# A two-part kernel on one core: first rows, GpSimd's DMA queue and the order of the last tables

## The chip, the cores and the metric

The kernel runs on one core of a Trainium2 chip. Its time is the device time of one execution in microseconds (us); for several runs the median is given. The core has five engines, each with its own program order: PE (TensorE: matmuls, transposes), DVE (VectorE), ACT (ScalarE), POOL (GpSimd) and SP (SyncE, which here only issues DMAs). SP, ACT and POOL issue DMAs, each in its own order: an instruction that waits holds up all that stands behind it on its engine. Sixteen DMA engines move the data for all of them.

## What is computed

The output has two halves side by side. The left half is an attention layer with a memory that is carried from segment to segment; the right half is a long convolution whose kernel comes from a state space model.

```python
# a: 64 segments of 32 rows, one after the other, 32 heads of 128
for s in range(n_seg):
    h = concatenate([mem, x[:, s*32:(s+1)*32]])          # 8 + 32 rows
    q, k, v = h @ Wq, h @ Wk, h @ Wv
    p = softmax(where(mask, q k^T * scale, -1e9))
    o = (p v) @ Wo
    mem = o[:, :8];  outs.append(o[:, 8:])
# b: convolution of u (2048 x 1024) with a kernel of 128 modes per column
K = real(sum_n C_n * exp(dt*A_n * l) * dt*B_n)           # l = 0..2047
y = irfft(rfft(pad(K)) * rfft(pad(u)))[:2048] + u * Dskip
return concatenate([a, b], axis=-1)
```

## The kernel before

**Part b comes first** (`part_b`, L699). It works in four stages, and parts of part a that do not depend on the recurrence are woven into them.

1. The parameter stage (the loop over `PAR`, L944) computes from A, B, C and log_dt the logarithms of the modes, split into three bfloat16 parts each, and stores them to the DRAM tensor `PB` (`part_put`, L883). The words of `PAR` set the order on every engine: T/c turn x's last rows, F/f build Fourier matrices `MF`, P/e are projections of part a (`Ahead.projections`, L140) and their evictions.
2. The loop over f from 0 to 15 (L1308) makes the tables and the convolution kernel's values, one block of 64 columns a pass. The words of `FIRST` (pass 0) and `ORDER` (the others) give the order: X..p and X..t are matmuls of the parameters, which `load_par` (L1029) brings from `PB` into one of two tiles `pt`, four DMAs a pass, one pass ahead, called in `exp_` (word E0); E is the exponential on ACT, n, S, b, C, w, gi, gr the sines and products on ACT and DVE, K and x the values and their copy into `KxT`. Woven in are U (`side`, L997: u's spectra on PE; every fourth eviction ends in `classes`, six operations on POOL and a 1 MB store to `Ud`), M (turned matrices, a store to `MId` from POOL), P (projections), R (`other_rows`, L114: x's other rows turned and stored to `VXd` by SP, L135).
3. After the passes 7 and 15, `put_values` (L1065) queues 44 stores of half of the kernel's values to `Kd` in a list `late`. One is taken out at each E (L1245), eight a pass, and issued by SP; those of the second half go out together after the loop (L1385), by POOL except the four largest, which stay with SP. In the tail (L1344 to L1389) the last tables are finished, and the turned columns `G` of the first blocks are built (`build`, L1162) and multiplied with the values that `load_k` (L1079) reads back from `Kd`.
4. The loop over b from 0 to 15 (L1509) multiplies the spectra block by block (`pointwise`, L1408) with u's, which `load_u` (L1196) loads through SP, and from b=4 on transforms back (`inverses`). At b=2 SP loads the second half of `Kd`. Part a's weights are loaded in the same loop (`resident`).

**Part a** (`part_a`, L266) then runs its 64 segments, streaming the weights that do not fit into SBUF; it is not touched.

The projections' outputs go by way of a list of their own, `Ahead.late`: `PKd` stores (eight for each finished group, L210) and `VXd<-PVd` copies, of which up to `burst` are issued before each eviction (L188, L201). PSUM tiles for the woven work come from `take` (L729), three buffers in turn. Where GpSimd's DMAs keep their descriptors is set small (`SCRATCH = 512`, L1580), to leave the room to weights.

Of the kernel before, what the change touches and what calls it, by code (L numbers as in the profile page):

```python
# [74 lines left out]
class Ahead:  # L75
# [38 lines left out]
    def other_rows(self, take, pool, ident):  # L114
# [11 lines left out]
        for b in range(NB):  # L126
# [5 lines left out]
            def evict(copy, b=b, pt=pt):  # L132
                xst = pool.tile([128, 4, self.KC, self.XM], BF16, name="xst", tag="xst", bufs=1)
                copy(out=xst[:].rearrange("p s k r -> p k s r"), in_=pt[:, :, 0:n].rearrange("p k (s r) -> p k s r", r=self.XM))
                nc.sync.dma_start(out=self.VXd[4 * b:4 * b + 4, :, 256:].rearrange("s p f -> p s f"), in_=xst[:].rearrange("p s k r -> p s (k r)"))  # L135
                if b + 2 < NB:
                    load(b + 2)
            yield evict

    def projections(self):  # L140
# [13 lines left out]
        self.burst = 0  # L154
# [20 lines left out]
        for i, (m, t, c) in enumerate(slices):  # L175
# [3 lines left out]
            for j in range(2):  # L179
                a = take([128, 512], F32, "pro")  # L180
                if m == "v":
# [5 lines left out]
                    def evict(copy, a=a, t=t, c=c, j=j):  # L187
                        for _ in range(min(self.burst, len(late))):  # L188
                            (late.pop(0) or skip)()
# [5 lines left out]
                else:  # L195
# [4 lines left out]
                    def evict(copy, a=a, m=m, t=t, g=g, h=h2 + j, mo=mo):  # L200
                        for _ in range(min(self.burst, len(late))):  # L201
# [6 lines left out]
                        def out():  # L208
                            for r in range(8):
                                late.append(lambda r=r: nc.sync.dma_start(out=PKd[8 * r:8 * r + 8, :, mo:mo + 128].rearrange("s p f -> p s f"),  # L210
                                                                          in_=st[:, 8 * r:8 * r + 8].rearrange("p s a b c -> p s (a b c)")))
# [457 lines left out]
def bcast_front(ap, n):  # L669
# [20 lines left out]
FIRST = ("X0p' X0t' U0 X1p E0 n0 X1t u0 U1 X2p E1 n1 X2t u1 P0 X3p E2 n2 X3t p0 U2 X4p E3 n3 X4t u2 U3 X5p E4 n4 X5t u3 P1 X6p E5 n5 X6t p1 "  # L690
         "X7p E6 n6 X7t E7 n7 P2 S0 p2 S1 P3 R p3 r M m P4").split()
# [3 lines left out]
       "f20 lo6/ F21 q4 P12 at e11/ b1 F22 P13 b2 f21 f22 b3 e12 F23 hi4 P14 q3 f23 e13 s4 hi3 F24 F25 e14/ P15 mi4 s3 f24 lo4 mi3 F26 P16 "  # L695
       "f25 lo3 e15 f26 F27 F28 f27 P17 e16 F29 e17 P18 f28 f29 F30 F31 f30 P19 f31 e18 P20 e19 e20").split()


def part_b(ctx, tc, u, A_re, A_im, B_re, B_im, C_re, C_im, log_dt, Dskip, out_b, ahead, copies, residents, first_state):  # L699
# [20 lines left out]
    v.memset(magic[:], MAGIC)  # L720
    ahead.open(ahead.ctx)
# [4 lines left out]
    ps_k = ctx1.enter_context(tc.tile_pool(name="b_psk", bufs=3, space=PSUM, side="right"))  # L726
# [11 lines left out]


# [13 lines left out]
    with tc.tile_pool(name="b_par", bufs=1) as par, tc.tile_pool(name="b_parh", bufs=2) as parh, \  # L753
# [129 lines left out]
        def part_put(k, i):  # L883
            q, row = {"1": (0, 0), "4": (0, 3), "2": (1, 0), "3": (1, 3), "6": (1, 6)}[k]
            sy.dma_start(out=PB[q][row + i].rearrange("(p t) n -> p t n", t=8), in_=parts[k, i][:])
# [23 lines left out]
        def ttx(word, eng, *args):  # L909
# [16 lines left out]
            "rp": powers_rows, "rt": phase_rows}  # L926
# [102 lines left out]
    def load_par(sb, eng=gp):  # L1029

        for q in range(2):
            n = 4 * PARTS[q]
            for h in range(2):
                eng.dma_start(out=par_t[sb % 2][ROW0[q] + n * h:ROW0[q] + n * h + n],
                             in_=PB[q][:].rearrange("c (q g s h e) n -> q s h c g e n", q=2, g=4, s=8, h=2)[sb // 8][sb % 8][h])
        return par_t[sb % 2]

# [24 lines left out]
    def put(out, in_):  # L1062
        late.append(lambda eng=sy: (sy if out.shape[1] == 32 else eng).dma_start(out=out, in_=in_))

    def put_values(sb):  # L1065
        kx = KxT["t"]
        for g in range(4):
            dsl = slice(512 * (sb // 8) + 128 * g, 512 * (sb // 8) + 128 * g + 128)
            for p0, u0, cols in ((0, 0, ((8, 1, 32),)), (8, 256, ((8, 2, 16),)), (16, 384, ((4, 1, 4), (8, 4, 8), (40, 1, 4))),
# [140 lines left out]
    pars = {0: load_par(0, sc)}  # L1210
# [27 lines left out]
    def exp_(r, e):  # L1238
# [6 lines left out]
        if late:  # L1245
            late.pop(0)()
# [56 lines left out]
    for eng, names in ((sc.copy, ON_ACT), (v.tensor_copy, ON_DVE)):  # L1303
        for nm, kind, slot in names:
            evict_of[nm] = (kind, slot, eng)
    TURNED = {"P0": 2, "P1": 0, "P2": 3, "P3": 1}
    steps = columns_of_turns()
    for f in range(16):  # L1308
        ahead.burst = 3 if f == 0 else 2
# [4 lines left out]
        if f == 15:  # L1314
# [5 lines left out]
            ks = [load_k(0, XT[:, 0:2048], 0)]  # L1320
            G.update({0: part_of(g0, 0), "rhs": g0[0:7, 5120:7168], "wts": g0[0:7, 7168:7552], "basis": g0[0:7, 7552:8064], "lhs": XT[0:7, 2048:3456]})
            G.update({kc: part_of(XT, 5120 * kc) for kc in (1, 2, 3)})
        for word in ORDER if f else FIRST:
# [3 lines left out]
            elif f == 15 and nm[0] == "P":  # L1327
                if nm in TURNED:
# [15 lines left out]
    wsl = [ahead.pool.tile([128, 2048], BF16, name="wq", tag="wsl", bufs=4) for _ in range(4)]  # L1344
    amps = [wsl[0][:, 0:1536], wsl[3][:, 0:1536]]
    uq = [t_[:].bitcast(F32) for t_ in wsl[1:3]]
    load_u(0)
    ks[0] += load_k(0, XT[:, 4096:4608], 4)
    made = [build(kc, lambda: take([128, 512], F32, "gf"), amps[kc]) for kc in range(2)]
# [4 lines left out]
    now = [[ps_e.tile([128, 2, 512], F32, name="pa", tag="pa")[:].rearrange("p h (c d) -> p h c d", c=2)] for _ in range(2)]  # L1354
    first = [XT[:, lo:lo + 4096].bitcast(F32).rearrange("p (a b c d) -> p a b c d", a=2, b=2, c=2) for lo in (15360, 10240)]

    def times_u(s_, Y, Z, n_):
        us = uq[n_].rearrange("p (a c d) -> p a c d", a=2, c=2)
        for i, t_ in ((1, Z), (0, Y)):
            v.tensor_tensor(out=t_[:, n_], in0=us[:, :, i, :].unsqueeze(2).to_broadcast([128, 2, 2, DQ]), in1=s_[n_][0], op=ALU.mult)  # L1360
# [3 lines left out]
    cosine(15, 0)  # L1364
    imaginary(15, 0)
    weighted(0, 0, amps[0])
    absolute(15, 1)
    spectrum(0, 0, [now[0][0][:, half] for half in range(2)])
    cosine(15, 1)
    minus(15, 1)  # L1370
    imaginary(15, 1)
    make(0, 5)
    real(15, 0)
    times_u(now, *first, 0)
    weighted(0, 1, amps[0])
    spectrum(0, 1, [now[1][0][:, half] for half in range(2)])
    make(1, 4)
    real(15, 1)
    for t in range(2):
        values(15, t)  # L1380
    times_u(now, *first, 1)
    for t in range(2):
        table_ops["x"](15, t)
    make(1, 10)
# [10 lines left out]
    Dsk = const.tile([128, D], BF16, name="Dsk")  # L1395
    sy.dma_start(out=Dsk[:], in_=Dskip.partition_broadcast(128))
# [11 lines left out]
    def pointwise(b, s_):  # L1408
        kc, Bt = b % 4, Bs[b // 4]
        Y, Z = (pw.tile([128, 2, 2, 2, DQ], F32, name=nm, tag=nm)[:] for nm in "yz") if b else first  # L1410
# [319 lines left out]
```

## Time and profile before

| | |
|---|---|
| median of 3 runs | 1983.08 us (1977.25 to 1986.69) |
| the profiled execution | 1991.66 us, span 1989.9 us |
| mean granted TensorE clock | 0.973 |
| busy: PE, DVE, ACT, POOL | 93%, 69%, 48%, 21% of the span |
| parameter stage | 0 to about 66 us |
| loop over f | about 76 to 386 us |
| tail, up to the last values | about 386 to 420 us |
| loop over b and back transforms | about 420 to 660 us |
| part a | about 660 to 1990 us |

Times in all profile lines are of the profiled execution, in us from the start of its span. In a timeline a line is: start, time, engine, source line, operation, out<-in, shapes, count, and in brackets the idle time of the engine before it and what ended it ("issue" means that no semaphore explains the wait). POOL's DMA issues stand under POOL, those of SP and ACT under SPq and ACTq. In the list of waits a line is: who waited for whom, total us, times, longest us. In a table of windows each engine has its busy time and, in brackets, its instructions.

### The profile page before, as it was taken

Reading aid. Unit: us, or ns where it says so; the run is one execution under the profiler, and the core shown is the slowest. Engines: PE = TensorE matmul, PEld = TensorE weight load, DVE = VectorE, ACT = ScalarE, POOL = GpSimd, SP = SyncE. Lnnn points to the kernel's source line nnn. Section 1 sums busy time; section 2 is a strip of 40 time slices with the busy share of each in tenths; the row PEclk is TensorE's granted clock in tenths of the full one; section 3 lists DMA queues with packets and bytes.
Section 4 is the critical chain, followed back from the end, with each engine's and each line's share of the span. In section 5 each row is a group of like instructions: output and inputs, shape, how many; then the busy total and the mean of one; then the engine's idle time right before and its main releaser. Section 6 shows DMA issues by size and latency. Waiting matters only on the chain.

```text
span 1989.9 us, 74737 instructions
## 1 busy us (share of the span) xinstructions
PE 1846.9 (93%) x32044; PEld 1134.5 (57%) x32044; DVE 1370.6 (69%) x3399; ACT 949.3 (48%) x1678; POOL 411.1 (21%) x859
## 2 busy tenths in 40 slices
PE   8799999778999799999999999999999999999999
PEld 3566666446887355555555555555555555555554
DVE  8499999858994466666666676666666666666650
ACT  8599999841223344343444444444444343434330
POOL 2254535224000111111111111111121111111120
PEclk9899999868999799999999999999999999999999
DMA  7789888757578899999999999999999999999991
GB/s 223 207 239 272 238 242 256 199 152 249 179 226 297 311 345 319 340 345 324 346 344 347 347 343 341 342 340 339 338 338 348 338 341 352 331 334 343 333 345 39
DMA packets 329350, 588.70 MB, mean 296 GB/s; under 512 B 86830, under 2 KB 202990, under 8 KB 326970
## 3 DMA queue, kind: packets, MB, share of 16 engines
q1 hardware_dynamic: 275592, 529.03, 78.3%
q10 hardware_dynamic: 45682, 29.82, 4.9%
q0 software_dynamic: 7744, 25.07, 3.5%
q8 instruction: 251, 4.11, 0.8%
q14 instruction: 81, 0.66, 0.1%
HBM read 528.25 MB, written 66.05 MB: 299 GB/s over the span
## 4 chain that ended last, share of the span: by engine, by line
PE 37%; DMA 24%; DVE 3%; issue 1%; ACT 1%; POOL 0%; ACTq 0%; POOLq 0%; SPq 0%; DVEq 0%
PE acc L404 20%; DMA wst<-WD_v 10%; PE pp L517 8%; DMA wst<-WD_o 6%; DMA wst<-WD_k 4%; DMA arena<-PKd 3%; PE pe L654 3%; PE tr L415 2%; DMA wst<-WD_q 1%; PE pv L485 1%; PE pv L489 1%; DVE arena L611 1%; PE sc L429 1%; ACT arena L611 1%; DVE arena L470 1%
## 5 line engine op out<-in xcount | busy, mean ns | idle before, releaser
L404 PEld LDWEIGHTS <-a_hT 128*32 128x32 bf16 x12352 | 329.7, 96 | 316.7 <-issue 62.6
L410 ACT CAST arena<-acc 128x512 bf16<-128x512 f32 x384 | 224.7, 585 | 402.0 <-PE acc L404 324.6
L517 PEld LDWEIGHTS <-arena 128*32 128x32 bf16 x8256 | 216.8, 97 | 86.3 <-issue 62.6
L404 PE MATMUL acc<-wst,a_hT 128*32 128x512 bf16 x2304 | 229.4, 382 | 26.0 <-DMA wst<-WD_v 17.6
L418 POOL COPY arena<-arena 128x128 bf16<-128x128 bf16 x128 | 37.3, 292 | 839.2 <-DMA arena<-PKd 278.6
L325 DVE TENSOR_SCALAR arena<-keep 128x256 int32<-128x256 int32 (+1 forms) x512 | 175.7, 395 | 31.5 <-PE acc L404 30.9
L404 PE MATMUL acc<-XM,a_hT 128*32 128x512 bf16 x2560 | 185.8, 381 | 0.0
L517 PE MATMUL pp<-W_o,arena 128*32 128x256 bf16 x3584 | 123.4, 274 | 6.9 <-DMA W_o<-in_A_Wo_dram 6.3
L444 DVE TENSOR_REDUCE a_mx<-sc 128x4 f32<-128x160 f32 (+1 forms) x192 | 71.6, 373 | 78.8 <-PE sc L432 78.8
L197 PE MATMUL pro<-XM,wsl 128*128 128x512 bf16 x512 | 122.3, 382 | 3.8 <-DVE kst L206 2.2
L448 ACT ACTIVATE sc<-sc 128x160 f32<-128x160 f32 (+1 forms) x192 | 63.9, 333 | 124.2 <-DVE sc L445 123.9
L404 PE MATMUL acc<-W,a_hT 128*32 128x512 bf16 x1536 | 118.6, 381 | 0.0
L532 DVE COPY arena<-tr 128x512 bf16<-128x512 bf16 x64 | 27.2, 425 | 127.7 <-PE tr L415 127.7
L452 DVE TENSOR_REDUCE a_mx<-sc 128x4 f32<-128x160 f32 (+1 forms) x192 | 72.9, 379 | 55.3 <-ACT sc L448 54.9
L1252 DVE TENSOR_SCALAR nr<-ptt 128x456 f32<-128x456 int16 x128 | 80.4, 628 | 38.6 <-PE ptt L1230 35.5
L1469 PE MATMUL yp<-Bt,MI 128*128 128x256 bf16 x680 | 104.5, 273 | 0.0
L404 PE MATMUL acc<-g,a_hT 128*32 128x512 bf16 x1024 | 101.8, 380 | 0.0
L479 POOL TENSOR_TENSOR arena<-arena,a_BD 128x128 bf16<-128x128 bf16 x128 | 51.0, 399 | 229.7 <-DVE arena L462 222.7
L1244 ACT ACTIVATE E<-pa 128x648 bf16<-128x648 f32 x128 | 87.9, 713 | 16.8 <-PE pa L1236 14.2
L611 ACT CAST arena<-pp 128x128 bf16<-128x128 f32 x64 | 17.0, 265 | 164.7 <-DVE arena L611 164.7
L404 PE MATMUL acc<-wq,a_hT 128*32 128x512 bf16 x1024 | 90.8, 382 | 0.0
L517 PE MATMUL pp<-wst,arena 128*32 128x256 bf16 x1536 | 76.5, 275 | 15.2 <-DMA wst<-WD_o 13.1
(332 smaller groups left out, 4048.3 us busy)
## 6 DMA issues: line engine op xcount, KB each, us to landing
wst<-WD_v SPq DMA_DIRECT2D x256, 512.0 KB
wst<-WD_k SPq DMA_DIRECT2D x192, 512.0 KB
wst<-WD_o SPq DMA_DIRECT2D x192, 512.0 KB
wst<-WD_q SPq DMA_DIRECT2D x128, 512.0 KB
Ud<-ux POOLq DMA_DIRECT2D x16, 1024.0 KB, 7.9
wq<-Ud SPq DMA_DIRECT2D x32, 512.0 KB
wsl<-in_A_Wk_dram SPq DMA_DIRECT2D x16, 512.0 KB
wsl<-in_A_Wv_dram SPq DMA_DIRECT2D x16, 512.0 KB
```

The lines of the kernel that those rows point to most:

```text
L197: nc.tensor.matmul(a[:], lhsT=w[:, kc, 128 * j:128 * j + 128], rhs=xTl[:, kc, :, :].rearrange("p s k -> p (s k)"), start=(kc == 0), stop=( ...
L325: nc.vector.tensor_scalar(out=out.bitcast(I32), in0=in_.bitcast(I32), scalar1=0, scalar2=None, op0=ALU.bitwise_or)
L404: nc.tensor.matmul(a[32 * g:32 * g + 32, o_:o_ + rhs.shape[1]], lhsT=hT[:, kc, :], rhs=rhs, start=(kc == 0), stop=(kc == KC - 1), tile_pos ...
L410: nc.scalar.copy(out=q, in_=a[:])
L444: nc.vector.tensor_reduce(out=m_, in_=x, axis=AX.X, op=ALU.max)
L448: nc.scalar.activation(out=flat(sc, i), in_=flat(sc, i), func=ACT.Exp, scale=scale)
L452: nc.vector.tensor_reduce(out=m_, in_=x, axis=AX.X, op=ALU.add)
L517: nc.tensor.matmul(po[32 * qt:32 * qt + 32, o_:o_ + rhs.shape[1]], lhsT=oT[:, h % 4, (h % 16) // 4, :], rhs=rhs, start=False, stop=(h == 3 ...
L654: nc.tensor.matmul(pe[n][:], lhsT=left[2 * b + hi // 16][:, 128 * (hi % 16):128 * (hi % 16) + 128], rhs=wo[u][:, 1024 * hh + 512 * n:1024 ...
L1244: sc.activation(out=T["E", r, e // 4][:, lo:lo + 8 * NE].rearrange("p (i c) -> p i c", i=2), in_=T.pop(("p", r, e))[:, :, 0:4 * NE], func= ...
L1252: v.tensor_scalar(out=T["n", r, e // 4][:, lo:lo + 8 * NT], in0=T.pop(("t", r, e))[:, 0:8 * NT].bitcast(I16)[:, 0:16 * NT:2], scalar1=floa ...
L1469: pe.matmul(yp[:, b, :], lhsT=m_[:, b, cs, kc, :], rhs=Bt[:, kc, j, half, c_, :], start=(kc == 0 and cs == 0 and half == 0), stop=(kc == 3 ...
```

## The change

In the parameter stage, the loads of the first rows (`load_par(0)`, before by ACT after the stage) become two words `ld0` and `ld1` of `PAR`, issued by POOL as soon as their parts are stored; the last parts 3 and 6 are stored by ACT instead of SP. `FIRST` starts with U0 U1 P0 and has its words in another order.

x's columns (`other_rows`) are stored to `VXd` by POOL, in two DMAs of two segments each instead of one of four by SP. All stores to `Kd` go by POOL, those of the first half too, one at each E; the widest (32 columns) is split into two of 16, so that there are 48 in each half instead of 44. While `PKd` stores are queued, one more is issued at each eviction.

In pass 15 the read-back of `Kd`'s first half and the load of u for block 0 are issued at the beginning of the pass; filler matmuls (`warm`) stand where the projections were. The tail has a new order: builds of all four `G` blocks use the two buffers `amps`, each step of a build is followed by a filler matmul, the products of block 0 are rotated and the spectra of block 1 taken ahead of the last values, and block 2 is built before the loop over b; block 3 is built at b=1. Dskip is loaded in pass 8 and serves as the fillers' operand. The diff is cut; in its part on the tail several calls stand on one line, with some arguments left out.

```diff
@@ other_rows
-                nc.sync.dma_start(out=self.VXd[4 * b:4 * b + 4, :, 256:].rearrange("s p f -> p s f"), in_=xst[:].rearrange("p s k r -> p s (k r)"))
+                for i in (0, 2):
+                    nc.gpsimd.dma_start(out=self.VXd[4 * b + i:4 * b + i + 2, :, 256:].rearrange("s p f -> p s f"),
+                                        in_=xst[:, i:i + 2].rearrange("p s k r -> p s (k r)"))
@@ projections
-                        for _ in range(min(self.burst, len(late))):
+                        for _ in range(min(self.burst + (self.keys > 0), len(late))):
                             (late.pop(0) or skip)()
...
+                            def put(r):
+                                self.keys -= 1
+                                nc.sync.dma_start(out=PKd[8 * r:8 * r + 8, :, mo:mo + 128].rearrange("s p f -> p s f"),
+                                                  in_=st[:, 8 * r:8 * r + 8].rearrange("p s a b c -> p s (a b c)"))
+                            self.keys += 8
                             for r in range(8):
-                                late.append(lambda r=r: nc.sync.dma_start(...))
+                                late.append(lambda r=r: put(r))
@@ words
-FIRST = ("X0p' X0t' U0 X1p E0 n0 X1t u0 U1 X2p E1 n1 X2t u1 P0 X3p E2 n2 X3t p0 U2 X4p E3 n3 X4t u2 U3 X5p E4 n4 X5t u3 P1 X6p E5 n5 X6t p1 "
-         "X7p E6 n6 X7t E7 n7 P2 S0 p2 S1 P3 R p3 r M m P4").split()
+FIRST = ("U0 U1 P0 X0p' X0t' X1p u0 E0 n0 X1t X2p u1 E1 n1 X2t X3p p0 E2 n2 X3t U2 X4p E3 n3 X4t P1 X5p E4 n4 u2 X5t U3 X6p E5 n5 p1 X6t "
+         "X7p E6 n6 u3 X7t P2 E7 n7 S0 R p2 S1 P3 r p3 M m P4").split()
 PAR = (...
-       "... f24 lo4 mi3 F26 P16 f25 lo3 e15 f26 ...
+       "... f24 lo4 ld0 mi3 F26 P16 f25 lo3 ld1 e15 f26 ...
@@ part_b
+    def load_par(sb, qs=(0, 1)):
+        for q in qs:
+            n = 4 * PARTS[q]
+            for h in range(2):
+                gp.dma_start(out=par_t[sb % 2][ROW0[q] + n * h:ROW0[q] + n * h + n],
+                             in_=PB[q][:].rearrange("c (q g s h e) n -> q s h c g e n", q=2, g=4, s=8, h=2)[sb // 8][sb % 8][h])
+        return par_t[sb % 2]
...
-            sy.dma_start(out=PB[q][row + i].rearrange("(p t) n -> p t n", t=8), in_=parts[k, i][:])
+            (sc if k in "36" and i == 2 else sy).dma_start(out=PB[q][row + i].rearrange("(p t) n -> p t n", t=8), in_=parts[k, i][:])
...
-        late.append(lambda eng=sy: (sy if out.shape[1] == 32 else eng).dma_start(out=out, in_=in_))
+        late.append(lambda eng=sy: eng.dma_start(out=out, in_=in_))
...
-            for p0, u0, cols in ((0, 0, ((8, 1, 32),)), (8, 256, ((8, 2, 16),)), (16, 384, ((4, 1, 4), (8, 4, 8), (40, 1, 4))),
+            for p0, u0, cols in ((0, 0, ((8, 1, 16), (24, 1, 16))), (8, 256, ((8, 2, 16),)), (16, 384, ((4, 1, 4), (8, 4, 8), (40, 1, 4))),
...
-    pars = {0: load_par(0, sc)}
+    pars = {0: par_t[0]}
...
         if late:
-            late.pop(0)()
+            late.pop(0)(gp)
...
+    def warm(n, t_):
+        for _ in range(n):
+            pe.matmul(t_[:], lhsT=ident[:], rhs=Dsk[:, 0:512], start=True, stop=True)
...
+        if f == 8:
+            sy.dma_start(out=Dsk[:], in_=Dskip.partition_broadcast(128))
...
-            ks = [load_k(0, XT[:, 0:2048], 0)]
+            wsl = [ahead.pool.tile([128, 2048], BF16, name="wq", tag="wsl", bufs=4) for _ in range(4)]
+            amps = [wsl[0][:, 0:1536], wsl[3][:, 0:1536]] * 2
+            uq = [t_[:].bitcast(F32) for t_ in wsl[1:3]]
+            ks = [load_k(0, XT[:, 0:2048], 0) + load_k(0, XT[:, 4096:4608], 4)]
+            load_u(0)
...
             elif f == 15 and nm[0] == "P":
+                warm(4 if nm in TURNED else 8, take([128, 512], F32, "wm"))
@@ the tail, its order before and after
-    absolute(15, 0); minus(15, 0); make(0, 9); cosine(15, 0); imaginary(15, 0); weighted(0, 0); absolute(15, 1); spectrum(0, 0)
-    cosine(15, 1); minus(15, 1); imaginary(15, 1); make(0, 5); real(15, 0); times_u(0); weighted(0, 1); spectrum(0, 1); make(1, 4)
-    real(15, 1); values(15, 0); values(15, 1); times_u(1); x(15, 0); x(15, 1); make(1, 10)
+    absolute(15, 0); minus(15, 0); make(0, 9); imaginary(15, 0); absolute(15, 1); minus(15, 1); imaginary(15, 1); make(0, 3)
+    weighted(0, 0); warm(3); spectrum(0, 0); make(0, 2); weighted(0, 1); spectrum(0, 1); cosine(15, 0); cosine(15, 1); times_u(0)
+    real(15, 0); times_u(1); real(15, 1); make(1, 9); values(15, 0); values(15, 1); make(1, 5); weighted(1, 0); spectrum(1, 0)
+    rotate(0); rotate(1); x(15, 0); x(15, 1); weighted(1, 1); spectrum(1, 1); make(2, 14)
     for f_ in late:
         f_(gp)
@@ the loop over b
+        if b == 0:
+            now = nxt_
-                if b == 0:
-                    next(points, None)
-                if b < 2:
-                    make(b + 2, (9, 5)[n_])
+                if b == 1:
+                    make(3, 7)
+                elif b == 2:
+                    warm(8, idle)
```

## The prediction

> **What bounds the kernel now.** I first read the windows of the whole span. From 660 us on PE and the DMA engines are both above 0.9 busy and the chain that ended last lies wholly there; the change does not touch that stage, which begins when the first stage ends. So the change is worth what it does to the moment at which the block products (the loop over b, from L1509) end. Three stretches of the first 480 us matter. The first is the end of the parameter stage, read in windows of 5 us (columns: length, PE, PEld, DVE, ACT, POOL busy, granted clock, DMA share, GB/s):
>
> ```profile
> 60.00:65.00 5.00, 5.00 (x41) 3.75 (x41) 0.00 (x0) 3.46 (x7) 2.10 (x4) 1.00 0.99 302
> 65.00:70.00 5.00, 1.39 (x13) 0.99 (x11) 0.00 (x0) 0.84 (x2) 0.31 (x1) 0.93 1.01 246
> 70.00:75.00 5.00, 0.00 (x0) 0.00 (x0) 0.00 (x0) 1.28 (x1) 0.00 (x0) 0.50 0.71 195
> 75.00:80.00 5.00, 4.02 (x19) 2.53 (x20) 0.92 (x2) 1.91 (x3) 0.00 (x0) 0.55 0.39 85
> ```
>
> PE stands still for nearly 10 us and comes back at half clock. The list of waits names the cause (pt<-PB), and the same list names what this prediction turns on:
>
> ```profile
> POOL pt L1034 <- issue: 65.2, 14, 6.4
> ...
> PE pa L1207 <- DMA XM<-Kd: 9.8, 1, 9.8
> PE pa L1236 <- DMA pt<-PB: 9.6, 1, 9.6
> ```
>
> The second stretch is the loop over f, about 95 to 386 us: PE is busy 48.7 of 50 us, so it is PE's, at 18.84 us a pass. POOL, hardly "busy", has little room in it. Its timeline for one pass:
>
> ```profile
> 240.16 1.26 POOL L991 TENSOR_TENSOR ux<-us 128x512 f32<-128x512 f32 x1 [3.15 <-DVE us L1020]
> ...
> 245.81 0.57 POOL L995 DMA_DIRECT2D Ud<-ux  x1 [0.42 <-POOL ux L994]
> 246.47 1.31 POOL L986 DMA_DIRECT2D MId<-ms  x1
> 247.77 1.13 POOL L1034 DMA_DIRECT2D pt<-PB  x2
> 254.86 1.07 POOL L1034 DMA_DIRECT2D pt<-PB  x2 [5.95 <-issue]
> 259.00 1.26 POOL L991 TENSOR_TENSOR ux<-us 128x512 f32<-128x512 f32 x1 [3.07 <-DVE us L1020]
> ```
>
> The third pt load waits 5.95 us with nothing to wait for but an earlier DMA: Ud, issued at 245.81, lands 7.9 us later by the median of the DMA issues. The tail shows the same with small stores, and what hangs on their end:
>
> ```profile
> 420.24 1.77 POOL L1063 DMA_DIRECT2D Kd<-KxT  x3 [34.59 <-ACT XM L1160]
> 424.19 3.77 POOL L1063 DMA_DIRECT2D Kd<-KxT  x7 [2.18 <-issue]
> 432.23 0.62 POOL L1063 DMA_DIRECT2D Kd<-KxT  x1 [4.27 <-issue]
> ...
> 458.59 1.07 POOL L1063 DMA_DIRECT2D Kd<-KxT  x2 [0.64 <-issue]
> ```
>
> SP's load of Kd's second half goes out at 461.96, when the last of these 40 stores has landed, and behind it in SP's order stands the load of u for block 4:
>
> ```profile
> 461.96 0.36 SPq L1081 DMA_DIRECT2D k<-Kd  x1
> ...
> 465.97 0.80 SPq L1198 DMA_DIRECT2D wq<-Ud  x2
> ```
>
> DVE waits for that load until 472.46. So POOL's stores already reach the path there.
>
> **A count that fits POOL's waits.** Give each POOL DMA its elements (from the code) divided by 16, by 8 where it covers eight partitions, by 6 or 9 for a pt load of 24 or 36 elements, plus one: Ud and MId of 128 elements 9 each; a pt load 5; a Kd store of 128 elements 17, of 64 9, of 32 5, of 16 3, the single row 2. Then never more than 31 are in flight. Ud, MId, pt, pt make 28, the next 5 would make 33: it waits till Ud lands. In the tail 17+5+9 = 31, and the next 5 waits for the 17 to land. The waits marked "issue" above all fit, so I take 31 places as the room. The count is my inference, not a row.
>
> **The change, part by part.** The sum is made against the profiled execution, 1991.66 us (span 1989.9), which is 8.6 us above the median of the runs, 1983.08.
>
> *First rows inside the parameter stage.* Gone from ACT: four issues, 4.68 us from 66.58. POOL's loads for rows 1 went out at 60.39 and 64.24; those places now belong to rows 0 and land, 4.6 to 7.3 us after issue by the two medians, at about 65 to 71 instead of 75.9. U0, U1, P0 (1.9 us each) run ahead of X0p', so PE works from 66.4 to 72. That is worth the 9.6 us wait and about 2 us of half clock on PE, but ACT's chain from the first E (76.7) to the second S (94.7) starts only some 4 to 6 us earlier and has 18 us to go, less 1 or 2 in a better order. Between 4 and 11, I take -8, since both chains gain. Behind ld0 and ld1, which wait on POOL for the parts to be stored, stand only the loads for rows 1, wanted a pass later. The last stores of parts 3 and 6 on ACT cost ACT about 0.8 us an issue, and what it evicts behind them waits for the subtraction; it is 70% busy there: 0 to 1 us.
>
> *x's columns by POOL.* SP loses one issue of 0.37 us a pass, which no engine waits for (PE's idle time in the loop is not wsl's): 0. POOL gets two stores of 256 elements, 17 places each: together 34, so the second waits until the first has landed, and everything behind it (MId, the next pass's pt loads, the next `classes`) queues. A pass of POOL becomes: 5.65 from the first ux to Ud's issue, 7.9 to its landing, 0.9 for the first half behind it, 0.3 and the second half's landing, 0.3, three more pt issues, 1.7. For that half no row exists; the nearest are the 32 KB Kd stores in the tail (2.6, 3.0, 3.7, 5.3, mean 3.6) and the 72 KB pt loads (4.6). With 4 the pass is 20.8 us against 18.84; with Ud at 5.5 and the half at 3.3 it is 17.7 and costs nothing. Eight passes: 0 to 16 us, less the 7 us by which pt lands ahead of X0p'. I take +3.
>
> *Kernel values by POOL.* The stores of the first half of Kd move from SP to POOL, eight in each pass from f=9 to 14, in groups of twelve worth 17,17,17,5,9,5,5,3,5,3,5,2 places. Each pass puts three behind the pt loads and ahead of `classes`, two between Ud and VXd, three behind VXd. No two 17s fit together, so each costs a landing, 3.6+0.3. Pass 9 and 12: 2.5 for pt, two landings 7.8 and an issue 0.6, `classes` 5.65, Ud 6 (the queues are emptier when PE waits), two VXd halves 0.3+3.9+3.9, MId and pt 2.8: 33.5. Pass 10 and 13: 2.5, 5.65, 6, then a 17, two halves, two 17s (0.9+0.3+15.6), pt 2.2: 33. Pass 11 and 14: 3.5, 5.65, 6, 0.3+7.8, 2.8: 26. POOL then sets the pass, because the pt loads of pass f+2 stand behind all this and PE's X0p' waits for them. Passes 9 to 13 are 14.7, 14.2, 7.2, 14.7, 14.2 over 18.84, 65; less 7 of lead, 58. With landings of 2.6 and Ud at 4.5 the passes are 28, 26 and 22 and the loss about 24; with 4.3 and 7.9 about 100. As the DMA engines are less loaded when PE waits, I lean to the light side: +52. If the stores cost only their issues, ten at 0.55 us, they would fit into the 9 us a pass that POOL idles: rival (a).
>
> The row for the landing of such a store is 2.6 to 5.3 us. [...]
>
> *f=15.* Extra PE work, 24 filler matmuls; and `gt` of P1 now waits for p0 on ACT: +3 (0 to 5). Loads of Kd and u ahead of the tables: the 9.8 us wait would go, but SP's load_k needs the last first-half store, which POOL issues late in its stretched pass 14, and SP's own load of u for block 0 queues behind load_k: both land about as late as before (404). I take +1, between -10 and +8.
>
> *The tail.* Builds and spectra move forward, some 70 fillers of 0.2 to 0.4 us keep PE's clock up where it was 0.5. All of it lies before b=4, where the u load of block 4 decides: it stands behind load_k of the second half, and that behind the last Kd store. The drain grows from 40 stores in 39.4 us to 48: per group three 17s at 3.9 and 6 for the rest (8.0, 4.1, 7.4, 4.4 before), 17.7, four groups 71: +31 (2.6-us landings: +12; 4.3: +40). The gains of the reordering are behind this and count nothing; without it they would be about 20 (the 9.8 us wait, and PE's half clock from 415 to 450 us). DVE then stands idle for tens of us ahead of block 4.
>
> *Rest.* Dsk earlier, one PKd store more an evict: 0.
>
> Sum: -8 +3 +52 +3 +1 +31 = +82, 2074 in the profiled execution, 2065 for the median.
>
> **Rivals.** (a) POOL takes the stores in its waits: the 5.95 and 3.07 us a pass are filled, no 17 waits. Then the front's 8 and the tail's 20 are kept: 1955. For it: POOL's busy share is 21%; against it: each "issue" wait ends with a landing. It decides if eight stores and two halves need less than the 9 us that POOL idles a pass. [...] (b) The room binds, but landings are as short as the shortest seen (1.6 to 2.6 us): -8 +24 +12, about 2000 to 2020 with smaller terms. (c) The first rows do not land earlier, because the stores of part 3 queue in full DMA engines (share 1.01 at 65 to 70): the front gives 0; 2073. (d) Loaded landings throughout: +100 and +40, 2120.
>
> **Chances.** The forecast with (c) and (d) 0.64, (b) 0.17, (a) 0.16, no change by cancelling 0.03. Half a percent, 10 us, is about what a measurement can tell. Faster 0.16, within 0.03, slower 0.81. Range 1995 to 2125: (b) to (d); the forecast's own is 2030 to 2105.
>
> **What would show it.** Right: passes of 18.8 us until f=8 and of 25 to 34 us from f=9 with PE waiting for pt<-PB at X0p'; POOL's "issue" waits grown from 65 us to some hundreds; Kd stores in the tail over 60 us; k<-Kd that much later and DVE waiting for wq<-Ud at block 4; the hole at 66 to 76 us gone. Wrong: POOL issuing Kd stores without waits, or two 17s in flight together.

## The result and the profile after

The changed kernel takes 2062.18 us (median; 2059.13 to 2067.08), the kernel before, on the same chip, 1983.08 (1977.25 to 1986.69): a ratio of 1.0396, with a 95% interval of 1.0369 to 1.0422. It is slower by 79 us, and the forecast was 2065. The profiled execution of the changed kernel took 2062.75 us (span 2061.0), 71.1 us more of span than the one of before.

Where these 71 us lie is read from moments that both kernels have: the issues of `Ud<-ux` by POOL (one a pass), SP's load of the second half of `Kd`, and SP's load of u for block 4 behind it.

| us from the span's start | before | after | difference |
|---|---|---|---|
| first Ud (pass 0) | 91.85 | 90.67 | -1.2 |
| ninth Ud (pass 8) | 245.81 | 246.70 | +0.9 |
| last Ud (pass 15) | 384.50 | 442.99 | +58.5 |
| first tail store of Kd by POOL | 420.24 | 476.32 | +56.1 |
| `k<-Kd` on SP | 461.96 | 537.23 | +75.3 |
| `wq<-Ud` for block 4 | 465.97 | 541.60 | +75.6 |
| end of the span | 1989.9 | 2061.0 | +71.1 |

So the passes 9 to 15 lose 57.6 us, and the way from the last Ud to block 4 loses 17.1 (98.6 against 81.5); the front gives almost nothing.

The end of the parameter stage in the profile after, in windows of 5 us (columns as in the prediction: length, PE, PEld, DVE, ACT, POOL busy, granted clock, DMA share, GB/s):

```profile
60.00:65.00 5.00, 4.40 (x24) 2.62 (x24) 0.00 (x0) 3.39 (x7) 3.31 (x6) 0.71 1.00 272
65.00:70.00 5.00, 5.00 (x41) 3.83 (x40) 0.00 (x0) 2.22 (x5) 1.26 (x3) 0.94 1.10 303
70.00:75.00 5.00, 5.00 (x44) 4.13 (x43) 0.18 (x1) 1.57 (x3) 0.00 (x0) 1.00 1.19 312
75.00:80.00 5.00, 3.11 (x20) 1.88 (x20) 3.45 (x6) 4.04 (x7) 0.00 (x0) 1.00 0.63 149
```

The hole of PE is gone and the clock is full at 70 to 80. But the projections of the stage now end at 70.8 us instead of 66.4, and POOL's adds for the first Ud start at 84.98 instead of 86.33.

The list of waits between 240 and 440 us (who waited for whom, total, times, longest), after:

```profile
PE ptt L1237 <- DVE nr L1259: 39.0, 15, 8.9
POOL Kd L1070 <- issue: 35.4, 11, 5.4
ACT sn L1264 <- DVE nr L1259: 28.8, 4, 9.0
POOL VXd L136 <- issue: 25.6, 8, 5.3
DVE ms L1001 <- DMA MId<-ms: 23.1, 4, 8.6
...
DVE xst L134 <- DMA VXd<-xst: 10.0, 2, 8.8
```

PE waits for DVE, and DVE waits for buffers (`ms`, `xst`) whose stores POOL issues late. No wait of PE for `pt<-PB` stands in this list. What POOL does in pass 8 and the beginning of pass 9 is seen in its timeline:

```profile
246.70 0.58 POOL L1011 DMA_DIRECT2D Ud<-ux  x1 [0.42 <-POOL ux L1010]
247.41 0.93 POOL L136 DMA_DIRECT2D VXd<-xst  x1
253.66 0.72 POOL L136 DMA_DIRECT2D VXd<-xst  x1 [5.32 <-issue]
254.38 0.55 POOL L1002 DMA_DIRECT2D MId<-ms  x1
...
260.79 0.64 POOL L1070 DMA_DIRECT2D Kd<-KxT  x1 [2.87 <-ACT E L1251]
265.63 1.46 POOL L1070 DMA_DIRECT2D Kd<-KxT  x1 [4.20 <-issue]
270.66 0.61 POOL L1070 DMA_DIRECT2D Kd<-KxT  x1 [3.57 <-issue]
271.29 1.28 POOL L1007 TENSOR_TENSOR ux<-us 128x512 f32<-128x512 f32 x1
```

Three stores of 17 places follow each other here, the second and the third each 0.3 us after the landing of the one before (4.5 and 4.7 us after its issue), and the adds of `classes` (271.29), which pass 9's Ud needs, stand behind them: 30.1 us from Ud to Ud instead of 18.8. The next intervals are 25.6, 32.6, 34.0, 23.5, 32.9 and 17.6. With the prediction's count of places, none of POOL's DMAs in this trace goes out while more than 31 places are taken, its own included.

POOL's time from the ninth to the last Ud, added up from its rows, shows where the 57.6 us come from. Its adds take 36.6 us before and 37.2 after, its DMA issues 25.6 and 62.7, its waits marked "issue" 29.0 and 67.4, and its waits for other engines 47.1 and 28.2. So the issues grew by 37 us and the waits for room by 38, and POOL had only 19 us of other waiting to give up for them.

The tail, POOL first:

```profile
476.32 0.65 POOL L1070 DMA_DIRECT2D Kd<-KxT  x1 [23.53 <-DVE KxT L1063]
481.08 0.61 POOL L1070 DMA_DIRECT2D Kd<-KxT  x1 [4.11 <-issue]
484.04 1.71 POOL L1070 DMA_DIRECT2D Kd<-KxT  x3 [2.35 <-issue]
...
532.55 3.79 POOL L1070 DMA_DIRECT2D Kd<-KxT  x7 [0.98 <-issue]
```

and then SP and DVE:

```profile
537.23 0.36 SPq L1088 DMA_DIRECT2D k<-Kd  x1
...
541.60 0.80 SPq L1205 DMA_DIRECT2D wq<-Ud  x2
```

```profile
547.54 1.22 DVE L1377 TENSOR_TENSOR z<-wq,hps 128x1024 f32<-128x1024 f32 x1 [22.49 <-DMA wq<-Ud]
```

The last of 48 stores has gone out 60 us after the first; block 4's products wait for it, DVE idle for 22.49 us.

### The profile page after: what moved, and what is told of

Read it like the earlier page. It is cut to its first block, busy times and chain, and to the rows that moved or that the text cites. A ratio compares the mean times of both kernels' runs of the same rounds, so it can differ in the third digit from the quotient of the medians.

```text
span 2061.0 us, 74976 instructions
## 1 busy us (share of the span) xinstructions
PE 1886.4 (92%) x32143; PEld 1138.7 (55%) x32143; DVE 1399.1 (68%) x3401; ACT 955.6 (46%) x1678; POOL 461.3 (22%) x951
## 4 chain that ended last, share of the span: by engine, by line
PE 36%; DMA 23%; DVE 3%; issue 1%; ACT 1%; POOL 0%; ACTq 0%; SPq 0%; POOLq 0%; DVEq 0%
PE acc L410 21%; DMA wst<-WD_v 8%; DMA wst<-WD_o 7%; PE pp L523 7%; DMA wst<-WD_k 3%; PE pe L660 3%; DMA arena<-PKd 2%; PE tr L421 2%; DMA wst<-WD_q 2%; PE sc L435 1%; DVE arena L617 1%; PE pv L495 1%; PE pv L491 1%; ACT arena L617 1%; PE tro L623 1%
## 5 line engine op out<-in xcount | busy, mean ns | idle before, releaser
L199 PE MATMUL pro<-XM,wsl 128*128 128x512 bf16 x512 | 131.1, 402 | 9.6 <-DVE us L1037 6.9
L199 PEld LDWEIGHTS <-wsl 128*128 128x128 bf16 x512 | 50.6, 102 | 85.1 <-issue 35.6
```

The lines of the kernel that those rows point to most:

```text
L199: nc.tensor.matmul(a[:], lhsT=w[:, kc, 128 * j:128 * j + 128], rhs=xTl[:, kc, :, :].rearrange("p s k -> p (s k)"), start=(kc == 0), stop=( ...
```

## The experiments

The theory, "places": POOL's DMAs share a room of 31 places, a store that does not fit waits for a landing, and from pass 9 on POOL's order, with these waits in it, sets the pass and in the tail block 4. Its rivals: the time is the transfers' own, whatever the queue; it is the number of POOL's DMAs; or it is DVE, which waits in order for the single buffers `ms` and `xst` and stands still beside POOL's adds. In all short diffs the lines with "-" are the changed kernel's or those of the kernel named.

The table gives the same moments for all runs, from their profiled executions, with the median and the ratio to the kernel before on the same chip (95% interval); in the runs of the experiments the kernel before had medians of 1984.99 to 1987.22.

| run | second Ud | ninth Ud | last Ud | `k<-Kd` | block 4's `wq<-Ud` | median, ratio |
|---|---|---|---|---|---|---|
| before | 112.47 | 245.81 | 384.50 | 461.96 | 465.97 | 1983.08 |
| after | 111.61 | 246.70 | 442.99 | 537.23 | 541.60 | 2062.18, 1.0396 (1.0369 to 1.0422) |
| loop's Kd stores on SP | 112.74 | 248.03 | 386.33 | 481.55 | 486.12 | 2008.36, 1.0123 (1.0077 to 1.0170) |
| x's columns on SP | 108.39 | 241.90 | 403.33 | 499.64 | 504.18 | 2023.68, 1.0190 (1.0163 to 1.0217) |
| tail's 8 widest on SP | 111.66 | 248.24 | 444.49 | 518.89 | 523.42 | 2043.56, 1.0298 (1.0266 to 1.0330) |
| all three on SP | 106.68 | 240.01 | 373.40 | 444.10 | 447.89 | 1975.17, 0.9943 (0.9908 to 0.9978) |
| 48 small DMAs, columns on POOL | 112.50 | 249.67 | 412.35 | 510.38 | 515.07 | 2034.48, 1.0232 (1.0203 to 1.0262) |
| 48 small DMAs, all three on SP | 109.58 | 242.90 | 379.35 | 457.40 | 462.03 | 1982.57, 0.9974 (0.9940 to 1.0008) |
| reduction instead of tensor-scalar | 110.41 | 248.19 | 444.44 | 536.46 | 541.26 | 2064.19, 1.0377 (1.0340 to 1.0415) |
| two buffers for ms | 112.50 | 248.71 | 446.90 | 537.18 | 541.62 | 2067.81, 1.0402 (1.0370 to 1.0434) |
| room of 1024 bytes | 106.78 | 240.69 | 379.27 | 451.34 | 455.17 | 1976.37, 0.9958 (0.9929 to 0.9987) |
| front alone | 107.88 | 241.56 | 376.12 | 454.49 | 458.30 | 1980.06, 0.9970 (0.9946 to 0.9994) |
| all three and 12 of the tail on SP | 108.41 | 241.73 | 377.12 | 442.72 | 450.65 | 1970.26, 0.9917 (0.9888 to 0.9945) |
| the same without fillers | 108.66 | 241.98 | 376.44 | 435.70 | 443.88 | 1962.21, 0.9885 (0.9841 to 0.9928) |

### The loop's stores of Kd back on SP

```diff
         if late:
-            late.pop(0)(gp)
+            late.pop(0)()
```

> The loop's stores of Kd (passes 9 to 14) go out on SP again; x's columns and the tail stay on POOL. Places (my theory: POOL's DMAs share 31 places, and POOL sets the pass): passes 9 to 14 come back to about 19 us, 50 to 58 us of the 79 go, 2004 to 2012 us. DMA number (it is the number of POOL's DMAs a pass, not their places): the same 48 stores leave, so the same. Columns (the two halves of x's columns alone hold POOL): only 10 to 30 us go, 2030 to 2050. The tail's drain stays at 60 us in all of them.

Measured: 2008.36 us. Ninth to last Ud takes 138.3 us instead of 196.3, as before the change (138.7): without these 48 stores the loop's 58 us are gone, and measured by the kernel before, the columns that stay on POOL hold up nothing there (the run with all three on SP will show 4.9 us). The tail is as slow as in the changed kernel (63 us from the first store to the last landing, 61 there). Number and places are not told apart by this run.

### x's columns back on SP

```diff
-                for i in (0, 2):
-                    nc.gpsimd.dma_start(out=self.VXd[4 * b + i:4 * b + i + 2, :, 256:].rearrange("s p f -> p s f"),
-                                        in_=xst[:, i:i + 2].rearrange("p s k r -> p s (k r)"))
+                nc.sync.dma_start(out=self.VXd[4 * b:4 * b + 4, :, 256:].rearrange("s p f -> p s f"), in_=xst[:].rearrange("p s k r -> p s (k r)"))
```

> x's columns go out on SP in one DMA again, Kd's stores stay on POOL. Places, by the terms of the forecast: a pass of POOL loses two halves' landings and an issue, 8.4 us, so passes 9 and 12 are 25, 10 and 13 are 24.6, 11 and 14 are 18.8: the loss of 58 falls to 24 less 7 of lead, 17, and passes 1 to 8 lose nothing: 2015 to 2035. Kd alone (Kd's stores hold POOL by themselves): 2050 to 2062. DVE's buffers (DVE waits in order for ms and xst until POOL's late stores land, and stands while POOL computes): the 10 us for xst go and part of the 23 for ms, the five stalls of 4 to 6 us beside POOL's adds stay: 2030 to 2045.

Measured: 2023.68 us, inside the range of places and outside that of Kd alone and of DVE's buffers. Ninth to last Ud is 161.4 us: measured by the kernel before, Kd's stores alone lose 22.7, the columns alone none (run above), both together 57.6. The two together cost far more in one queue than what each costs alone, added up. The run also moves the second Ud from 111.61 to 108.39 and the ninth from 246.70 to 241.90: the columns cost 4.8 us up to pass 8.

### The tail's widest stores on SP

```diff
     for f_ in late:
-        f_(gp)
+        f_(gp, sy)    # the eight stores of 16 columns of the first eight rows go by the second queue
```

> Only in the tail, the eight widest stores of Kd (16 columns of the first eight rows, 17 places each) go out on SP, the other 40 on POOL. Places: the drain falls from 60 us to about 40, as before the change, and block 4 comes 17 to 22 us earlier: 2040 to 2046 us. If the drain isn't what block 4 waits for, nothing: 2060. If the stores on SP are as slow there (the transfers, not the places, take the time): 2055 to 2062.

Measured: 2043.56 us. Eight of 48 stores on SP, and the drain is 42 us (first store to last landing) instead of 61. SP's timeline in this run shows what these eight cost there, and block 4's load at 523.42 instead of 541.60:

```profile
476.50 4.39 SPq L1070 DMA_DIRECT2D Kd<-KxT  x8
...
518.89 0.36 SPq L1088 DMA_DIRECT2D k<-Kd  x1
...
523.42 0.80 SPq L1205 DMA_DIRECT2D wq<-Ud  x2
```

Eight issues in 4.39 us, none of them waiting. The drain is what block 4 waits for, and 18.2 us of it were these stores.

### All three on SP

The edits of the three runs together; the front, the new orders, the early builds and the fillers stay.

> All three together: x's columns, the loop's stores of Kd and the tail's widest stores on SP; the first rows in the parameter stage, the order of the first pass, the early builds and the fillers stay. Places: what is left of the change is the front (1 to 2 us), the tail up to the drain (2 to 3 us) and a drain as before: 1975 to 1983 us. If the reordered tail's 20 us count after all: 1955 to 1965. If the early builds and fillers cost: 1985 to 2000.

Measured: 1975.17 us, a little faster than before (0.9943). Of the 18 us at block 4, 5.8 are there at the second Ud, 5.3 more come between the ninth and the last, and 7 in the tail (74.5 us from the last Ud to block 4's load instead of 81.5). The profiled execution, 1966.1 us, is 9 us faster than the run's median, so the 18 us are more than the medians show. By these, what the change has besides POOL's stores is a gain of about 10 us, and the stores cost some 87.

This run is also the better measure for the loop, since it has the new front and orders: ninth to last Ud takes 133.4 us. Of the 5.3 us less than before, 3.9 are in passes 11 and 12, which took 21.3 and 20.1 us in the profiled execution of before and 18.8 and 18.7 here. By 133.4, the columns alone (138.3) cost 4.9 us, Kd's stores alone (161.4) 28.0, and both together 62.9.

### Forty-eight small DMAs beside the stores on SP

```diff
-            late.pop(0)(gp)
+            late.pop(0)()
+            gp.dma_start(out=Kq.pop(0)[:], in_=ident[0:1, :])    # 48 scratch rows of 256 bytes
```

> As the run with the loop's Kd stores on SP, and beside each of them POOL issues one DMA of a single row of 256 bytes (2 places, into a scratch tensor that nothing reads): 48 more POOL DMAs in passes 9 to 14, as many as in the changed kernel, with few places. Places: they cost next to nothing, 2008 to 2016 us. Number or issue time of POOL's DMAs (0.55 us each, eight a pass): the loss is back, 2045 to 2062.

Measured: 2034.48 us, between the two ranges, so neither expectation held, that of places included. 48 DMAs of two places cost 24.4 us between the ninth and the last Ud (162.7 against 138.3). The likely account is issue time: with the columns on it POOL has little slack in a pass (its waits for other engines are 11.2 us of the 138.3 in the run above), and 48 x 0.55 is 26. POOL's waits marked "issue" fit this, with 53.1 us here and 57.3 there. But the run does not show it alone. The small DMAs take places too, and MId then waits behind them (23 places are taken, and its 9 would make 32):

```profile
305.26 1.52 POOL L1255 DMA_DIRECT2D Kq<-b_ident  x3
310.81 0.58 POOL L1003 DMA_DIRECT2D MId<-ms  x1 [4.03 <-issue]
```

And the 24.4 us are not spread evenly over the passes: three DVE instructions of 1.10 us are held for 5.1 to 5.3 us beside POOL's adds, of which a later section tells. Whether a DMA costs by itself, or only a queue without slack makes it cost, was left open and tested with the columns on SP:

```diff
# against the run with all three on SP
             late.pop(0)()
+            gp.dma_start(out=Kq.pop(0)[:], in_=ident[0:1, :])
```

> As the run with all three POOL moves undone (1975), and beside each of the loop's Kd stores on SP one DMA of 256 bytes by POOL, as in the run that gave 2034 with x's columns on POOL (26 us for 48 of them, 0.55 each). Places and pass: without the columns POOL idles 9 us a pass, eight issues of 0.55 fit in, 1970 to 1980. If each POOL DMA costs by itself whatever the room: 26 us again, 1998 to 2004.

Measured: 1982.57 us, a little above the expected range; by the trace the loop loses 3.1 us (136.5 against 133.4) instead of 24.4. Against that run 2.9 us more are lost before the second Ud and 8.2 in the tail, where the two kernels have the same code; the intervals of the two ratios overlap, and this is not explained. So 48 small DMAs are nearly free where POOL idles (3.1 us), and cost 24.4 us in a POOL that holds the columns too.

### A larger room

```diff
-SCRATCH = 512
+SCRATCH = 1024
-LOW = (("half", (1024,)), ...
+LOW = (("half", (768,)), ...
```

The rest of the edit is not shown. To make the memory free, the kernel leaves out 256 columns of block 7 of the query weights and uses another block's in their place.

> The changed kernel with 1024 instead of 512 bytes a partition set aside for POOL's descriptors. To make room in SBUF a quarter of one half block of the query weights (256 columns of block 7) is taken from another block, so that output is not the reference's; the work of every engine is the same but for a few more matmuls in the last stage. Places (512 bytes hold 31 and one spare of 16 bytes, 1024 hold 63): POOL's pass of 5.65 for the adds and some 9.5 for sixteen issues fits in 18.8, 45 to 58 of the loop's 58 us go, the tail's 48 stores take 48 issues of 0.57, 27 us instead of 60: 1972 to 1995 us, and more than 31 places in flight. If the transfers and not the room take the time (bytes, DMA engines): 2045 to 2062, and still 31 at most.

Measured: 1976.37 us, 86 us less than the changed kernel, with every store where the change put it. Up to 63 places are in flight in this trace, never more, by the same count that gives 31 at 512 bytes. POOL's timeline behind the Ud of pass 10, where three stores of 17 places and the two halves of the columns go out:

```profile
278.14 0.58 POOL L1012 DMA_DIRECT2D Ud<-ux  x1 [0.30 <-POOL ux L1011]
278.71 2.01 POOL L1071 DMA_DIRECT2D Kd<-KxT  x2
280.72 2.23 POOL L136 DMA_DIRECT2D VXd<-xst  x2
288.25 0.64 POOL L1071 DMA_DIRECT2D Kd<-KxT  x1 [5.30 <-issue]
289.26 1.15 POOL L1071 DMA_DIRECT2D Kd<-KxT  x2 [0.38 <-issue]
290.41 0.60 POOL L1003 DMA_DIRECT2D MId<-ms  x1
291.00 1.66 POOL L753 DMA_DIRECT2D pt<-PB  x3
```

A 17 (the second store at 278.71) and two halves stand in flight together with Ud, 62 places, and the next 17 waits 5.30 us. Ninth to last Ud is 138.6 us, as before the change, and the drain of the tail, all 48 on POOL, takes 38.4 us instead of 61.1 (27 expected, which counted the issues alone). POOL's order, the number of its DMAs and their bytes are the same as in the changed kernel: what changed is the room. From the ninth to the last Ud POOL's issues take 67.4 us here, no less than the 62.7 there, but its waits marked "issue" are 14.8 instead of 67.4. This decides for places, and against transfers that take the time by themselves and against the number of DMAs as a cause of its own. By the two traces block 4's load still comes 7.3 us later than with all three on SP (455.17 against 447.89); the medians, 1976.37 and 1975.17, do not show this.

### Two buffers for ms

```diff
-                ms = up.tile([128, 2, 4, 128], BF16, name="ms", tag="ms")
+                ms = up.tile([128, 2, 4, 128], BF16, name="ms", tag="ms", bufs=2)
-                        vst = vals.tile([128, 2, 2, 128], BF16, name="vst", tag="vst", bufs=6)
+                        vst = vals.tile([128, 2, 2, 128], BF16, name="vst", tag="vst", bufs=5)
```

> The changed kernel with two buffers for ms instead of one (and five for vst instead of six, to make room). DVE's 23 us of waiting for MId to land should go from the list. Buffers (that wait is what holds PE): 15 to 23 us faster, 2039 to 2047. Places (POOL sets the pass, and the wait moves to xst or to PE's pt): at most 10 us, 2052 to 2062.

Measured: 2067.81 us, no gain (the ratio is 1.0402 against 1.0396). The waits of this run between 240 and 440 us:

```profile
POOL VXd L136 <- issue: 38.2, 10, 7.0
PE ptt L1237 <- DVE nr L1259: 32.7, 14, 9.3
DVE xst L134 <- DMA VXd<-xst: 31.9, 5, 10.4
...
PE pa L1243 <- DMA pt<-PB: 8.2, 2, 5.4
```

The 23.1 us for `ms` are gone, those for `xst` grew from 10.0 to 31.9, and PE now waits for `pt<-PB` too. POOL is late, and whichever buffer comes first in DVE's order shows it; to free one buffer moves the wait. Two buffers for both were not tried.

### DVE beside POOL's adds

In the changed kernel a DVE instruction that takes 0.36 us elsewhere takes 5.83 where POOL's adds run beside it (271.29 to 276.5), and four more are stretched to between 4 and 6 us from then to pass 15. The first of them, and one that is free:

```profile
270.90 5.83 DVE L1277 TENSOR_SCALAR wn<-sn 128x768 bf16<-128x768 bf16 x1
...
302.81 0.36 DVE L1277 TENSOR_SCALAR wn<-sn 128x768 bf16<-128x768 bf16 x1
```

All five are tensor-scalar instructions, 0.36 or 1.10 us elsewhere and 4.09 to 5.83 here; `nr<-ptt`, a tensor-scalar instruction with its input in PSUM, takes 0.63 beside the adds as elsewhere. The author expected another form of instruction not to be held, which no run had shown. From pass 8 on this run makes |n| and -w with a one-element reduction:

```diff
+        if r >= 8:
+            n_ = T["n", r, h][:]
+            v.tensor_reduce(out=n_, in_=n_.unsqueeze(2), axis=mybir.AxisListType.X, op=ALU.max, apply_absolute_value=True)
+            return
...
+        if r >= 8:
+            v.tensor_reduce(out=wn[:], in_=turned(windows(T["s", r, h])).unsqueeze(3), axis=mybir.AxisListType.X, op=ALU.max, negate=True)
+            return
```

> [...] Places alone (the stalls lie beside POOL's lag): 2056 to 2064.

Measured: 2064.19 us, no gain. But the experiment did not take the stalls away as it should: beside the adds (364.18 to 369.4) now stands a product with two SBUF inputs, 1.11 us elsewhere, and it is held instead:

```profile
363.36 0.95 DVE L1282 TENSOR_REDUCE wn<-sn 128x768 bf16<-128x768 bf16 x1
364.22 6.15 DVE L1225 TENSOR_TENSOR gr<-E,nr 128x1824 bf16<-128x1824 bf16 x1
```

The stall went from one instruction to another (6.15 us for 1.11), and why the adds hold DVE was not shown. What the stalls are worth by themselves stays open: in the changed kernel these five add some 24 us to DVE's time, and no run takes them away while POOL is late. The run with the larger room shows that they go (one of 4.19 us is left) once POOL is on time.

### The front alone

The kernel before with `ld0`, `ld1`, the last stores of parts 3 and 6 on ACT and the new `FIRST`, and nothing else.

> The kernel before with the front alone: the two parts' loads of the first rows by POOL inside the parameter stage, the last stores of parts 3 and 6 on ACT, and the first pass's new order. My forecast gave 8 (4 to 11) us; the changed kernel's trace shows 1.2 at its first transform and the run with all POOL moves undone shows 5.8 at the second Ud. Front real, hidden by x's columns: second Ud at 106 to 109 against 112.5, 1977 to 1982 us. Front nothing: 1984 to 1988.

Measured: 1980.06 us, 0.9970 (0.9946 to 0.9994). The second Ud comes at 107.88 instead of 112.47, 4.6 us earlier, and block 4's load 7.7 us earlier; passes 11 and 12 take 18.7 us each here, 3.9 less in all than in the profiled execution of before. In the changed kernel the second Ud comes at 111.61: the second half of the columns waits 7.13 us ("issue") in pass 0, and the adds of pass 1 stand behind it.

### Twelve tail stores on SP, and no fillers

```diff
# against the run with all three on SP
-                    put(dst[:, at:at + n], ..., p0 == 0)
+                    put(dst[:, at:at + n], ..., n == 16)
# and in the second run
     def warm(n, t_):
-        for _ in range(n):
+        for _ in range(0):
```

> The best so far (all three POOL moves undone), with all twelve 17-place stores of the tail on SP instead of eight. Places: no 17 is left on POOL, so its drain is bound by 36 issues of 0.55 us and falls from 37 us to 20 to 27, and block 4 comes earlier until blocks 1 to 3 decide, 5 to 12 us: 1963 to 1970 us. If blocks 1 to 3 already decide, or SP's four more issues hold the u loads: 1975.

> The best so far (1970, twelve tail stores on SP) without the filler matmuls, all else the same. Clock: PE's granted clock in the 50 us before block 4 falls from 0.76 to 0.55 to 0.65, blocks 0 to 3 come 8 to 20 us later: 1978 to 1990. If DVE, ACT and the drain set that stretch: 1966 to 1974.

Measured: 1970.26 us for the first, whose drain is 29.9 us (20 to 27 expected) and no longer what SP waits for: `k<-Kd` goes out at 442.72, 2.8 us after the last landing. For the second 1962.21 us, where a loss was expected. PE and its clock from 390 to 450 us, with the fillers:

```profile
390.00:410.00 20.00, 18.50 (x208) 8.35 (x207) 12.85 (x16) 11.65 (x16) 0.00 (x0) 0.76 0.12 25
410.00:430.00 20.00, 20.00 (x95) 9.38 (x95) 11.86 (x11) 9.57 (x17) 15.45 (x28) 0.76 0.72 196
430.00:450.00 20.00, 20.00 (x97) 9.86 (x96) 15.06 (x15) 8.32 (x14) 4.40 (x8) 0.79 0.75 259
```

and without:

```profile
390.00:410.00 20.00, 16.33 (x204) 10.32 (x205) 16.08 (x19) 10.42 (x16) 5.09 (x10) 0.66 0.16 28
410.00:430.00 20.00, 15.54 (x79) 8.25 (x77) 13.24 (x12) 10.22 (x21) 12.79 (x24) 0.71 0.87 280
430.00:450.00 20.00, 15.44 (x90) 10.15 (x89) 18.21 (x16) 3.54 (x7) 7.75 (x15) 0.78 0.76 240
```

The clock is lower by 0.01 to 0.10 without fillers, yet DVE gets more done (47.5 us busy of 60 against 39.8), and block 4's load comes 67.4 us after the last Ud instead of 73.5. A likely cause, not shown, is that the fillers stand in PE's order ahead of work that ACT and DVE wait for (between 390 and 450 us DVE's waits for ACT fall from 12.5 to 7.5 us, those for PE only from 10.8 to 9.6). The intervals of the two ratios overlap (0.9888 to 0.9945 and 0.9841 to 0.9928), so a gain from leaving them out is likely and not shown; no run shows that they pay. The version without fillers is the fastest of this study, 0.9885 of the kernel before.

## Why the prediction was right, point by point

- **POOL's room** was right, and it was the term that made the sign. The count of 31, inferred from waits, is confirmed by a room twice as large with 63 and no loss.
- **Kd in the loop (+52), f=15 (+3) and the earlier loads (+1).** Ninth to last Ud lost 57.6 us against 56. The prediction counts a pass of POOL from the end of one pass's pt loads to the end of the next one's, so the intervals from Ud to Ud above are not its passes. Counted its way, passes 9 to 13 take 36.2, 32.4, 22.9, 34.3 and 34.3 us, where 33.5, 33, 26, 33.5 and 33 stood: 160.0 in all against 159. The same stretch took 96.4 us before, so 63.6 are lost there, 1.1 more ahead of it, and 7.1 come back between it and the last Ud; the sum had 65, less 7 of lead, and then leaned to 52. The parts were not all as counted: in these five passes POOL waits 20.6 us for DVE and ACT, for which the sum has nothing, so its waits for landings were shorter than counted, and that the totals agree so closely is in part luck. Nor are the landings the whole of the loss: POOL's issues grew by 37 us and its waits for room by 38. The run with the larger room has the same issues and, measured by the kernel before, loses nothing (138.6 against 138.7), so the issues cost only because the waits had used up POOL's idle time.
- **The waits.** POOL's waits marked "issue" were to grow from 65 us to some hundreds; in the whole span they are 81.3 for `VXd` and 68.4 for `Kd`, and those for `pt` fall to 20.2 (85 to 440 us): about 170 in all, fewer than forecast. The loss of the loop is larger than the growth of these waits there (from 29.0 to 67.4), since the issues grew too.
- **The route failed as a step.** "The pt loads of pass f+2 stand behind all this and PE's X0p' waits for them" is not what the trace shows: DVE waits 23.1 us for `ms` and 10.0 for `xst`, and PE for DVE. The size held because POOL sets the pass by any of these routes; with `ms` doubled the wait moves on to `xst` and to `pt`.
- **The front (-8).** By itself it gives 4.6 us at the second Ud and 7.7 at block 4 in its one trace, and some 6 by its ratio. In the changed kernel 1.2 are left of it at the first Ud and nothing at pass 8. The hole of PE was real and went, but the stage before ended 4.4 us later, and **x's columns (+3)** cost 4.8 up to pass 8. Together +0.9 at the ninth Ud instead of -5.
- **The tail (+31).** The term was mis-sized: 17.7 us for a group of twelve stores were counted, 15 measured (60.0 for four). Counted from the last Ud, the first tail store came 2.4 us earlier, and from the last Ud to block 4 the loss was 17.1 us. That the drain alone decides block 4, and that the reordering counts nothing behind it, was right: 8 stores moved gave 18.2 us back. That fillers keep the clock up was the author's estimate: from 390 to 450 us it was 0.76 to 0.79 with them (twelve tail stores on SP), 0.66 to 0.78 without, and 0.57 to 0.61 in the kernel before. What the reordering is worth without the drain was given as 20; 7 with the old drain and 14 with twelve stores on SP and no fillers were seen.
- **Rest (0).** After block 4 the changed kernel's span is 4.5 us shorter; no cause was looked for. In the other runs this stretch varies from 1512 to 1529 us.
- The sum in the profiled executions was +82 against +71.1. The median came out within 3 us only because the profiled execution of before lay 8.6 us above its median and that of after 0.6.
- **The rivals.** (a), 1955, fell: each wait ended with a landing. Of it remains that the change without POOL's stores is faster (1975, and 1962 at best). (b), short landings, is seen a little in the tail (15 us a group instead of 17.7) and not in the loop. (c) came near by its price, the front gave 1, but not by its cause: the first rows did land earlier and the hole went. (d) did not come.

## What to carry to other kernels

A DMA that moves to GpSimd's queue is not costed by its issue alone (0.60 us for a `Kd` store here, while the 96 of them waited 68.4 us, marked "issue"): count its places against the room that the kernel has set aside, and look at what stands behind it in POOL's order. A list of waits names the buffer that comes first, not the cause; if POOL's "issue" waits grow, freeing that buffer can move the wait and no more (with two buffers for `ms` its 23.1 us went and the wait for `xst` grew from 10.0 to 31.9). Before giving such a move up, try a larger room, if the memory for it can be found (1024 bytes instead of 512 took 86 us off the changed kernel). Fillers for the clock raised the clock by 0.01 to 0.10 here, and no run shows that they pay.

## What the runs showed of the hardware that was not expected

- The room for POOL's DMAs followed the bytes set aside: by the prediction's count of places, 512 bytes a partition held at most 31 and 1024 at most 63, one less than a place for each 16 bytes. The stores on POOL cost 87 us with the one (2062.18 against 1975.17 with the columns, the loop's stores and eight of the tail's on SP) and nothing that the medians resolve with the other (1976.37).
- Which queue issues a store mattered: 48 stores moved from POOL to SP took 54 us off the kernel, and eight in the tail 18.2 us off the way to block 4. A full room makes POOL wait (67.4 us marked "issue" between the ninth and the last Ud), and SP's eight went out in 4.39 us.
- POOL's adds held a DVE instruction for as long as the whole row of six ran (5.83 us for one of 0.36, beside a row of 5.2), not for one of them (1.3). In the kernel before, all 16 rows of adds fall on DVE instructions with an input in PSUM, none of which is longer than elsewhere (`nr<-ptt` 0.63 beside them, 0.62 free): the order of the words keeps the two apart, as long as POOL is on time.
